# Moving the sections of G, splits, conversion and the state tile to other steps of a two-network kernel, and asking for later weights a phase earlier

## The chip, the cores and the metric

The kernel runs on one core of a Trainium2 chip. The metric is the device time of one execution in microseconds (us). Three runs of the kernel before gave 1648.82, 1658.09 and 1655.11 us, a median of 1655.11 us.

## The reference, cut to what matters

Three stages follow each other: an attention between 512 positions and 32 state slots for 4 batches of 8 heads, a mixture of 8 experts with a doubly normalised gate, and a gated two-layer network.

```python
# x: (4, 8, 512, 64), state: (4, 8, 32, 64)
a = softmax(x @ state.T / 8);   xread = a @ state
a2 = softmax(state @ x.T / 8);  sread = a2 @ x
x = concat([xread, sread], axis=2)          # to (2176, 512)
# experts: w1 (8, 512, 1024), w2 (8, 1024, 512)
P = exp(x @ w_gate - max); 8 times: rows to sum 1, columns to sum 1, times N / E
out = sum over e of P[:, e:e+1] * (relu(x @ w1[e]) @ w2[e])
# second network: w_in (512, 2048), w_out (2048, 512)
h = out @ w_in;  y = (h * sigmoid(h)) @ w_out
```

Inputs and outputs are float32, the second network's weights 64-bit. The kernel splits each operand into a high and a low part and multiplies three times (`mm3`, lines 91 to 93: high by low, low by high, high by high), which keeps float32 accuracy.

## The kernel before, in words

**Tiles and units.** Tokens come in batches `b` = 0 to 3 of 512 positions (four tiles of 128) and one tile `B` = 4 with the 128 state rows, called the state tile here. Each expert's hidden width of 1024 is cut into two units of 512, so there are 16 units `u` of four sections `f` of 128. One step `(u, b, f)` has a first layer `S1` (6 matmuls into a bank of the pool `p1`, then `hh` on ScalarE, L706, and `hl` on VectorE, L707) and a second layer `S2` (12 matmuls, three for each of the batch's four tiles, into four banks of the pool `p2`, tiles `po`). After the fourth section VectorE adds the four banks, weighted by the gate, to the accumulators (L746). `S1` runs two steps (`LAG`) ahead of `S2`. Units 0 and 1 do all four batches in this way. From unit 2 (`UPE`) on a unit does batches 0 and 1 alone, in eight steps, k = 4 b + f; batches 2 and 3 of these units come later, in a loop of their own with seven products for eight, for which GpSimd, ScalarE and the queues prepare sums of second weights during the dense units (`w2_sum`, `w2_split`).

**G.** The attention's read is a product with the state, so the first layer multiplies the attention weights by G = state x w1, which `g_pieces` makes: for each of four sections `hp` of 128 inputs 6 matmuls of 64 rows, two at a time on the two halves of the array (L626), into two banks; ScalarE copies the banks to a staging tile (L630) and sends it to memory, from where `load_g` and `split_g` bring it back in another order. `g_pair(u, i)` does two of the four sections, and so needs both banks of `p1` and both banks of `pm`. At units 2 and later the two pairs for unit u + 2 stand inside `S2`, after its second tile, at steps 1 and 2 (`within`).

**The state tile.** `sr_first(u)` is its first layer, 12 matmuls at once into a bank of `p1`; `sr_turn` transposes and splits the result; `sread_second` runs its four `S2` of three matmuls each, in step 3, in a bank of `p2`.

**Weights.** `load_raws` asks for a unit's raw weights in one tile of the pool `s8`; `load_w1` and `load_w2` split one section of them, high part on ScalarE (L243), low part on VectorE (L96, tile `l_w`). First weights for unit u + 3 are split at steps 5, 6, 7 and 0, second weights at 1, 2 for this unit and at 1, 6 for the next.

**Conversion.** The second network's weights are 64-bit words. `convert_some` advances a generator that turns them into high and low parts, mostly by VectorE (L302 to L360), and stores them; `store` issues the stores that have been put off. It is called at steps 2, 4, 5 and 6, and in the second network for the last quarter of the weights.

**The second network.** 16 phases `(g, v, fp)`: two halves `g` of the tokens, four quarters `v` of the width, two parts `fp`. A phase has seven `step(p)` (`product`, 6 matmuls, and the load of the next phase's weights) and, between them, four pieces `second(q - 1, n)` of the phase before. In the first half the state tile's part is interleaved: `s_first(v, half)` with weights `wr` from `s_load(v, half)`, `s_back`, `s_second`. `load_wout` asks for second weights, in a pool with five tiles for each of the two parts.

**What sets the order.** TensorE runs in the order written. The other engines' orders are made when the kernel is built: among instructions that are ready, the one written first goes first; a queue then runs in that order, and an instruction that waits holds up what is behind it. `behind_rows` and `issue_after` keep casts and conversion behind the last `hh` or `hl` written so far. SyncE issues nearly all loads, and most stores, from one queue.

Of the kernel before, what the change touches and what calls it, by code (L numbers as in the profile page):

```python
# [21 lines left out]
def fused_kernel(ctx: ExitStack, tc: tile.TileContext, x, state, w_gate, w1, w2, w_in, w_out, out):  # L22
# [16 lines left out]
    B, H, S, D = x.shape  # L39
    NS = state.shape[2]  # L40
    DM = H * D
    E, _, F = w1.shape
# [7 lines left out]
    NF = FU // 128  # L50
    KD = DM // 128
    UPE = F // FU
    NU = E * UPE
    NV = F2 // FU
# [26 lines left out]
    def p2(name):  # L81
        return ps2.tile([128, 512], F32, tag="p2", name=name)
# [287 lines left out]
    for v in range(NV):  # L370
        for kp in range(2):
            for j in range(2):
                k = kp + 2 * j
# [242 lines left out]
    def g_pieces(u, hps, banks):  # L616

        lanes = [slice(64 * half, 64 * half + 64) for half in range(2)]
        pg = {}
        for hp, bank in zip(hps, banks):  # L620
            wh, wl = w1t[u, hp]
            for half in range(2):
                pg[hp, half] = bank(f"pg{u}_{hp}_{half}")
            for i, (a, w) in enumerate(((stl, wh), (sth, wl), (sth, wh))):
                for half in range(2):
                    nc.tensor.matmul(pg[hp, half], a[lanes[half], hp], w[lanes[half]], start=i == 0, stop=i == 2)  # L626
        for hp in hps:
            stg = stp.tile([128, 2, FU], F32, tag="stg", name=f"stg{u}_{hp}")
            for half in range(2):
                nc.scalar.copy(stg[:, half], pg[hp, half])  # L630
            c = 2 * (hp & 1)
            nc.scalar.dma_start(out=g_d[u][hp // 2, c:c + 2].rearrange("h p f -> p h f"), in_=stg)
# [17 lines left out]
    def g_pair(u, i):  # L650
        if i == 0:
            g_start(u)
        g_pieces(u, (2 * i, 2 * i + 1), (pm, p1))

# [63 lines left out]
    def S2(u, b, f, within=()):  # L718
        tiles = batches[b]
        if f == 0:  # L720
            s2p[u, b] = [p2(f"po{u}_{b}_{t}") for t in tiles]
        hh, hl = hT.pop((u, b, f))
# [280 lines left out]
    def s_load(v, half):  # L1003
        pool, tag = (s8, "s8") if v else (accp, "acc")
        t = wr[v, half] = pool.tile([128, 2, 2, FU], F32R, tag=tag, name=f"wr_{v}_{half}")
        nc.sync.dma_start(out=t.bitcast(F32), in_=wr_d[v][2 * half:2 * half + 2].rearrange("k p s f -> p k s f"))
# [76 lines left out]

    pair_at = {0: {8: (1, 0), 9: (1, 1)}, 1: {6: (2, 0), 8: (2, 1), 13: (3, 0), 15: (3, 1)}, 2: {3: (4, 0), 4: (4, 1)}}

# [44 lines left out]
    bal = balance()  # L1130
    for i in range(-LAG, len(steps)):
        if i + LAG < len(steps):
            S1(*steps[i + LAG])
        else:
            block(UPE, 0, 0, i + LAG - len(steps))
# [3 lines left out]
        if i >= 0:  # L1139
            u, b, f = steps[i]  # L1140
            k = b * NF + f
            at = pair_at.get(u, {1: (u + 2, 0), 2: (u + 2, 1)}).get(k)
            if at and at[0] >= NU:
                at = None
            S2(u, b, f, [lambda: g_pair(*at)] if at else [])
        if i < B * NF:
# [37 lines left out]
        if late and k in (0, 1):  # L1184
            load_w1(4, 2 * k)
            load_w1(4, 2 * k + 1)
        if u > UPE and k in (1, 2):
            load_w2(u, k + 1)
        if u > UPE + 1 and k == 0 and u + 2 < NU:
            load_w1(u + 2, 3)  # L1190
        if k == 3:
            sread_second(u)
        store()
        if more and not late and k in (2, 4, 5, 6):
            convert_some()
# [8 lines left out]
        if more:  # L1204
# [5 lines left out]
            if k == 6:  # L1210
                if u + 2 < NU:
                    load_raws(2, u + 2)
                if u + 4 < NU:
                    load_raws(1, u + 4)
            if k == (5 if late else 4) and u + 2 < NU:
                sr_first(u + 2)
            if k == 6:
                sr_turn(u + 1)
            if k == (4 if late else 1):
                load_w2(u + 1, 0)  # L1220
# [4 lines left out]
            if u + 3 < NU:  # L1225
                for hp in ({6: (0, 1), 7: (2, 3)} if late else {5: (0,), 6: (1,), 7: (2,)}).get(k, ()):
                    load_w1(u + 3, hp)
# [117 lines left out]
    for q, (g, v, fp) in enumerate(phases):  # L1345
# [3 lines left out]
        def step(p):  # L1349
            product(q, p)  # L1350
            if more:
                load_win(*phases[q + 1][1:], p)
            if q < 6:
                store()
                if p in (2, 7) or q and p in (1, 5):
                    convert_some(1)
            if q == 7 and p != 4:
                later = {1: 6, 5: 3, 2: 7, 6: 4}.get(p)
                if later:
                    tokens(1, later)  # L1360
# [12 lines left out]
        if q == 0:  # L1373
            load_wout(0, 0, 2)
            s_first(0, 1)
            s_load(1, 0)
        elif g == 0 and fp == 1:
            s_back(v)
        step(6)
        earlier[1]()  # L1380
        if s0 and q:
            s_first(v, 0)
            s_load(v, 1)
        step(3)
        step(7)
        earlier[2]()
        if s0 and q:
            s_first(v, 1)
            if v + 1 < NV:
                s_load(v + 1, 0)  # L1390
        step(4)
        earlier[3]()
        if q == 0:
            load_wout(0, 0, 3)
        if more:
            for f in range(2):
                g1, v1, fp1 = phases[q + 1]
                if q:
                    load_wout(g1, v1, 2 * fp1 + f)
        if q == 6:  # L1400
# [39 lines left out]
```

## Time and profile before

| what | value |
|---|---|
| median of three runs | 1655.11 us |
| lowest, highest | 1648.82, 1658.09 us |
| profiled execution, its time | 1654.59 us |
| its span, first to last instruction | 1652.8 us |
| mean granted TensorE clock | 0.996 |
| TensorE busy | 1615.0 us (98%) |
| VectorE busy | 1098.7 us (66%) |
| ScalarE, GpSimd busy | 724.6 us (44%), 652.0 us (39%) |

The profiled execution is one run of the program; its time is 1.8 us longer than its span, for what lies around the first and last instruction. Busy shares are means over stages: start-up to about 100 us, units 0 and 1 to about 250 us, dense units to about 820 us, the other batches of those units to about 1280 us, the second network to the end. A window's column of busy time is followed by the number of instructions in brackets; PEclk is the granted clock as a share of 2.4 GHz.

### The profile page before, as it was taken

Reading aid. Unit: us, or ns where it says so; the run is one execution under the profiler, and the core shown is the slowest. Engines: PE = TensorE matmul, PEld = TensorE weight load, DVE = VectorE, ACT = ScalarE, POOL = GpSimd, SP = SyncE. Lnnn points to the kernel's source line nnn. Section 1 sums busy time; section 2 is a strip of 40 time slices with the busy share of each in tenths; the row PEclk is TensorE's granted clock in tenths of the full one; section 3 lists DMA queues with packets and bytes.
Section 4 is the critical chain, followed back from the end, with each engine's and each line's share of the span. In section 5 each row is a group of like instructions: output and inputs, shape, how many; then the busy total and the mean of one; then the engine's idle time right before and its main releaser. Section 6 shows DMA issues by size and latency. Waiting matters only on the chain.

```text
span 1652.8 us, 21117 instructions
## 1 busy us (share of the span) xinstructions
PE 1615.0 (98%) x7269; PEld 1291.5 (78%) x7269; DVE 1098.7 (66%) x1672; ACT 724.6 (44%) x1231; POOL 652.0 (39%) x487
## 2 busy tenths in 40 slices
PE   7999999999999999999999999999999999999998
PEld 5778777777777777777878788888888778888887
DVE  8933793567566666666447777777777878764554
ACT  5643346444444444343344444444444433443332
POOL 1001124444334423343457786776654512222222
PEclk9999999999999999999999999999999999999999
DMA  7043367676668656666356565454442787555441
GB/s 185 16 149 91 115 211 271 236 237 210 207 231 267 217 200 218 227 206 221 102 157 172 174 167 161 133 178 149 129 148 77 259 276 257 169 159 168 141 140 68
DMA packets 196395, 293.50 MB, mean 178 GB/s; under 512 B 35584, under 2 KB 82240, under 8 KB 196288
## 3 DMA queue, kind: packets, MB, share of 16 engines
q1 hardware_dynamic: 169552, 242.71, 47.5%
q10 hardware_dynamic: 26736, 49.44, 8.0%
q8 instruction: 58, 0.95, 0.2%
q14 instruction: 49, 0.40, 0.1%
HBM read 194.27 MB, written 97.81 MB: 177 GB/s over the span
## 4 chain that ended last, share of the span: by engine, by line
PE 84%; DVE 10%; DMA 2%; issue 1%; ACT 1%; POOL 1%; SPq 0%; DVEq 0%; ACTq 0%; POOLq 0%
PE pBa L984 9%; PE po L91 8%; PE po L93 7%; PE po L92 7%; PE pBc L984 5%; PE pa L791 4%; PE ph L91 4%; PE ph L93 3%; PE ph L92 3%; PE pr L91 3%; PE pr L92 3%; PE pB L91 3%; PE pr L93 3%; PE pB L93 3%; PE pB L92 3%; PE pg L626 3%
## 5 line engine op out<-in xcount | busy, mean ns | idle before, releaser
L707 DVE SCALAR_TENSOR_TENSOR hl<-ph,hh 128x512 fp32r<-128x512 f32 x144 | 98.9, 687 | 212.2 <-ACT hh L706 211.8
L91 PE MATMUL po<-h_w,hl 128*128 128x512 f32 x576 | 230.6, 400 | 6.9 <-DVE acc L746 6.9
L93 PE MATMUL po<-h_w,hh 128*128 128x512 f32 x576 | 226.6, 393 | 0.0
L92 PE MATMUL po<-l_w,hh 128*128 128x512 f32 x576 | 226.3, 393 | 0.0
L706 ACT ACTIVATE hh<-ph 128x512 fp32r<-128x512 f32 x144 | 86.3, 599 | 279.3 <-PE ph L93 276.4
L96 POOL TENSOR_TENSOR gl<-sg,gh 128x512 fp32r<-128x512 f32 x64 | 86.8, 1358 | 261.3 <-ACT gh L824 254.4
L96 POOL TENSOR_TENSOR G<-gf,G 128x512 fp32r<-128x512 f32 x64 | 85.3, 1355 | 262.9 <-ACT G L667 231.6
L91 PEld LDWEIGHTS po<-h_w,hl 128*128 128x128 f32 x576 | 108.5, 188 | 43.1 <-issue 11.2
L96 POOL TENSOR_TENSOR T<-t,T 128x512 fp32r<-128x512 f32 x84 | 112.3, 1338 | 73.5 <-ACT T L947 73.0
L984 PE MATMUL pBa<-T,wh 128*128 128x512 f32 x448 | 139.4, 392 | 0.7 <-DVE T L96 0.7
L220 POOL TENSOR_TENSOR w2s<-w2s,w2h 128x512 fp32r<-128x512 f32 x56 | 79.8, 1426 | 149.1 <-ACT w2h L219 148.9
L93 PEld LDWEIGHTS po<-h_w,hh 128*128 128x128 f32 x576 | 108.5, 188 | 23.9
L92 PEld LDWEIGHTS po<-l_w,hh 128*128 128x128 f32 x576 | 108.8, 189 | 22.8 <-issue 0.2
L91 PE MATMUL ph<-aTh,G 128*128 128x512 f32 x288 | 118.1, 410 | 3.8 <-DVE hl L707 1.9
L947 ACT CAST T<-t 128x512 fp32r<-128x512 f32 x112 | 69.6, 621 | 115.0 <-DVE t L952 94.6
L92 PE MATMUL ph<-aTl,G 128*128 128x512 f32 x288 | 113.1, 393 | 0.8 <-DVE aTl L96 0.8
L93 PE MATMUL ph<-aTh,G 128*128 128x512 f32 x288 | 113.5, 394 | 0.0
L91 PE MATMUL pr<-woh,gl 128*128 128x512 f32 x256 | 100.6, 393 | 0.7 <-DVE res L850 0.7
L92 PE MATMUL pr<-wol,gh 128*128 128x512 f32 x256 | 100.2, 391 | 0.0
L93 PE MATMUL pr<-woh,gh 128*128 128x512 f32 x256 | 100.0, 391 | 0.0
L984 PEld LDWEIGHTS pBa<-T,wh 128*128 128x128 f32 x448 | 84.2, 188 | 19.9 <-DVE T L96 1.3
L791 PE MATMUL pa<-x,wi 128*128 128x512 f32 x372 | 98.0, 399 | 0.7 <-ACT u L795 0.7
(267 smaller groups left out, 3835.8 us busy)
## 6 DMA issues: line engine op xcount, KB each, us to landing
g_d<-stg ACTq DMA_DIRECT2D x60, 512.0 KB, 3.7
wi<-wi_d SPq DMA_DIRECT2D x108, 256.0 KB, 3.0
raw<-in_moe_w_dram SPq DMA_DIRECT2D x104, 256.0 KB, 5.1
gf<-g_d SPq DMA_DIRECT2D x128, 128.0 KB, 4.2
w_d<-w2h ACTq DMA_DIRECT2D x56, 256.0 KB, 3.0
w_d<-w2s SPq DMA_DIRECT2D x56, 256.0 KB, 2.2
gfs<-g_d SPq DMA_DIRECT2D x112, 128.0 KB, 4.0
wh<-w_d SPq DMA_DIRECT2D x56, 256.0 KB, 3.3
```

The source lines that it names most:

```text
L91: nc.tensor.matmul(ps, al, bh, start=first, stop=False)
L92: nc.tensor.matmul(ps, ah, bl, start=False, stop=False)
L93: nc.tensor.matmul(ps, ah, bh, start=False, stop=last)
L96: engine.tensor_tensor(out=lo, in0=src, in1=hi.bitcast(F32), op=ALU.subtract)
L220: nc.gpsimd.tensor_tensor(out=t.bitcast(F32R), in0=t, in1=hi.bitcast(F32), op=ALU.subtract)
L626: nc.tensor.matmul(pg[hp, half], a[lanes[half], hp], w[lanes[half]], start=i == 0, stop=i == 2)
L706: last["act"] = nc.scalar.activation(out=hh, in_=ph, func=AF.Relu)
L707: last["dve"] = nc.vector.scalar_tensor_tensor(out=hl, in0=ph, scalar=0.0, in1=hh.bitcast(F32), op0=ALU.max, op1=ALU.subtract)
L791: nc.tensor.matmul(ps, a, b, start=begin, stop=kp == 1 and i == 2, skip_group_check=True)
L947: nc.scalar.copy(hi, t)
L984: nc.tensor.matmul(ps, a, b, start=p in (1, 2, 5) and q == 0 and i == 0, stop=q == 1 and i == 2, skip_group_check=True)
```

## The change

Nothing that is computed changes. In the dense units: a pair of sections of G stands in front of the first layer that is issued in a batch's first step (steps 0 and 4, the second pair for unit u + 2 and the first for unit u + 3) and no longer inside S2 at steps 1 and 2; the order of its four banks is different; the state tile's second layer goes from step 3 to step 2 and into the pool `pm`; `sr_first` from step 4 to 1, `sr_turn` from 6 to 4; first weights are split at steps 2, 2, 5 and 6; second weights a step earlier, and one from step 1 to 4; conversion is called at steps 1, 2, 4 and 5. Unit 2 has times of its own. In the second network: half of the `wr` tiles come from the pool `acc`, and `wr` is asked for in the phase before; `load_wout` is called in the phase itself and not at the end of the phase before; the calls of conversion are spread over one more phase.

```diff
@@ -617,10 +617,10 @@
 
         lanes = [slice(64 * half, 64 * half + 64) for half in range(2)]
         pg = {}
-        for hp, bank in zip(hps, banks):
+        for n, hp in enumerate(hps):
             wh, wl = w1t[u, hp]
             for half in range(2):
-                pg[hp, half] = bank(f"pg{u}_{hp}_{half}")
+                pg[hp, half] = banks[n][half](f"pg{u}_{hp}_{half}")
             for i, (a, w) in enumerate(((stl, wh), (sth, wl), (sth, wh))):
                 for half in range(2):
                     nc.tensor.matmul(pg[hp, half], a[lanes[half], hp], w[lanes[half]], start=i == 0, stop=i == 2)
@@ -650,7 +650,7 @@
     def g_pair(u, i):
         if i == 0:
             g_start(u)
-        g_pieces(u, (2 * i, 2 * i + 1), (pm, p1))
+        g_pieces(u, (2 * i, 2 * i + 1), ((p1, pm), (pm, p1)))
 
     gf = {}
 
@@ -718,7 +718,7 @@
     def S2(u, b, f, within=()):
         tiles = batches[b]
         if f == 0:
-            s2p[u, b] = [p2(f"po{u}_{b}_{t}") for t in tiles]
+            s2p[u, b] = [(pm if b == B and u > UPE else p2)(f"po{u}_{b}_{t}") for t in tiles]
         hh, hl = hT.pop((u, b, f))
         wh, wl = w2t[u, f]
         for i, ps in enumerate(s2p[u, b]):
@@ -1001,7 +1001,7 @@
         sx["h"], sx["l"] = hi, lo
 
     def s_load(v, half):
-        pool, tag = (s8, "s8") if v else (accp, "acc")
+        pool, tag = (accp, "acc") if v == 0 or half else (s8, "s8")
         t = wr[v, half] = pool.tile([128, 2, 2, FU], F32R, tag=tag, name=f"wr_{v}_{half}")
         nc.sync.dma_start(out=t.bitcast(F32), in_=wr_d[v][2 * half:2 * half + 2].rearrange("k p s f -> p k s f"))
 
@@ -1081,7 +1081,9 @@
     first = {0: {4: [(1, 0), (1, 1)], 5: [(1, 2), (1, 3)], 9: [(0, 0), (0, 1)], 10: [(0, 2), (0, 3)], 14: [(1, 0), (1, 1)], 15: [(1, 2), (1, 3)]},
              1: {**{k: [(2, k - 2)] for k in range(2, 6)}, **{k: [(3, k - 9)] for k in range(9, 13)}}}
 
-    pair_at = {0: {8: (1, 0), 9: (1, 1)}, 1: {6: (2, 0), 8: (2, 1), 13: (3, 0), 15: (3, 1)}, 2: {3: (4, 0), 4: (4, 1)}}
+
+    pair_within = {0: {8: (1, 0), 9: (1, 1)}, 1: {6: (2, 0), 8: (2, 1), 13: (3, 0), 15: (3, 1)}}
+    pair_at = {0: {}, 1: {}, 2: {3: (4, 0), 4: (4, 1)}, 3: {0: (5, 0), 1: (5, 1), 4: (6, 0)}}
 
     ask_at = {0: {11: (1, 0), 13: (1, 1)}, 1: {0: (1, 2), 3: (1, 3), 11: (2, 0), 13: (2, 1)}}
     split_at = {0: {12: (1, 0), 15: (1, 1)}, 1: {2: (1, 2), 5: (1, 3), 13: (2, 0), 15: (2, 1)}}
@@ -1129,6 +1131,11 @@
 
     bal = balance()
     for i in range(-LAG, len(steps)):
+        if i >= 0:
+            u, b, f = steps[i]
+            at = pair_at.get(u, {0: (u + 2, 1), 4: (u + 3, 0)}).get(b * NF + f)
+            if at and at[0] < NU:
+                g_pair(*at)
         if i + LAG < len(steps):
             S1(*steps[i + LAG])
         else:
@@ -1137,12 +1144,8 @@
             for piece in early.get(i, ((), ()))[0]:
                 piece()
         if i >= 0:
-            u, b, f = steps[i]
-            k = b * NF + f
-            at = pair_at.get(u, {1: (u + 2, 0), 2: (u + 2, 1)}).get(k)
-            if at and at[0] >= NU:
-                at = None
-            S2(u, b, f, [lambda: g_pair(*at)] if at else [])
+            at = pair_within.get(u, {}).get(b * NF + f)
+            S2(*steps[i], [lambda: g_pair(*at)] if at else [])
         if i < B * NF:
             for piece in early.get(i, ((), ()))[1]:
                 piece()
@@ -1184,14 +1187,12 @@
         if late and k in (0, 1):
             load_w1(4, 2 * k)
             load_w1(4, 2 * k + 1)
-        if u > UPE and k in (1, 2):
-            load_w2(u, k + 1)
-        if u > UPE + 1 and k == 0 and u + 2 < NU:
-            load_w1(u + 2, 3)
-        if k == 3:
+        if u > UPE and k < 2:
+            load_w2(u, k + 2)
+        if k == (3 if late else 2):
             sread_second(u)
         store()
-        if more and not late and k in (2, 4, 5, 6):
+        if more and not late and k in (1, 2, 4, 5):
             convert_some()
         if late and k == 0:
             w2_sum(u, 4)
@@ -1212,18 +1213,18 @@
                     load_raws(2, u + 2)
                 if u + 4 < NU:
                     load_raws(1, u + 4)
-            if k == (5 if late else 4) and u + 2 < NU:
+            if k == (4 if late else 1) and u + 2 < NU:
                 sr_first(u + 2)
-            if k == 6:
+            if k == (6 if late else 4):
                 sr_turn(u + 1)
-            if k == (4 if late else 1):
+            if k == 4:
                 load_w2(u + 1, 0)
             if k == 6:
                 load_w2(u + 1, 1)
             if k in (3, 7):
                 split_g(u + 1, k // 7)
             if u + 3 < NU:
-                for hp in ({6: (0, 1), 7: (2, 3)} if late else {5: (0,), 6: (1,), 7: (2,)}).get(k, ()):
+                for hp in ({5: (0, 1), 6: (2, 3)} if late else {2: (0, 1), 5: (2,), 6: (3,)}).get(k, ()):
                     load_w1(u + 3, hp)
             at = k - 3 if late else k
             if at == 0:
@@ -1350,9 +1351,9 @@
             product(q, p)
             if more:
                 load_win(*phases[q + 1][1:], p)
-            if q < 6:
+            if q < 8:
                 store()
-                if p in (2, 7) or q and p in (1, 5):
+                if p in ((2, 7), *[(1, 2, 7)] * 4, *[(1, 5, 2, 7)] * 2, ())[q]:
                     convert_some(1)
             if q == 7 and p != 4:
                 later = {1: 6, 5: 3, 2: 7, 6: 4}.get(p)
@@ -1371,32 +1372,28 @@
         step(2)
         earlier[0]()
         if q == 0:
-            load_wout(0, 0, 2)
             s_first(0, 1)
-            s_load(1, 0)
         elif g == 0 and fp == 1:
             s_back(v)
+        if q:
+            load_wout(g, v, 2 * fp)
+        if g == 0 and fp == 1 and v + 1 < NV:
+            s_load(v + 1, 0)
         step(6)
         earlier[1]()
+        if q:
+            load_wout(g, v, 2 * fp + 1)
         if s0 and q:
             s_first(v, 0)
-            s_load(v, 1)
         step(3)
         step(7)
         earlier[2]()
         if s0 and q:
             s_first(v, 1)
-            if v + 1 < NV:
-                s_load(v + 1, 0)
+        if g == 0 and fp == 1 and v + 1 < NV:
+            s_load(v + 1, 1)
         step(4)
         earlier[3]()
-        if q == 0:
-            load_wout(0, 0, 3)
-        if more:
-            for f in range(2):
-                g1, v1, fp1 = phases[q + 1]
-                if q:
-                    load_wout(g1, v1, 2 * fp1 + f)
         if q == 6:
             for p, (pool, tag) in zip((1, 5, 2), ((s8, "s8"), (accp, "acc"), (accp, "acc"))):
                 tokens(1, p, pool, tag)
```

## Rows read from the trace of the kernel before

**Rows 1.** The page, part 1: span, busy time and instructions.

```profile
span 1652.8 us, 21117 instructions
PE 1615.0 (98%) x7269; PEld 1291.5 (78%) x7269; DVE 1098.7 (66%) x1672; ACT 724.6 (44%) x1231; POOL 652.0 (39%) x487
```

**Rows 2.** Waits of TensorE, whole span: total us, times, longest.

```profile
PE po L91 <- DVE acc L746: 8.6, 4, 2.7
PE psf L91 <- DMA wr<-wr_d: 3.5, 1, 3.5
PE ph L91 <- ACT stg L630: 0.9, 2, 0.6
```

**Rows 3.** Windows, one unit each: busy us (instructions) of each engine, PEclk, DMA.

```profile
432.20:475.20 43.00, 42.99 (x200) 33.79 (x198) 25.40 (x40) 19.79 (x36) 15.73 (x12) 1.00 0.69 233
561.20:608.50 47.30, 44.92 (x200) 34.88 (x198) 34.05 (x49) 19.41 (x36) 17.17 (x12) 0.96 0.64 211
```

**Rows 4.** Windows, unit 6: steps 1 to 4, step 5, steps 5 to 0.

```profile
429.00:455.00 26.00, 26.00 (x121) 19.84 (x120) 10.54 (x18) 11.21 (x20) 7.81 (x6) 1.00 0.61 211
455.00:459.20 4.20, 4.20 (x19) 3.39 (x19) 1.89 (x3) 3.16 (x5) 2.60 (x2) 1.00 0.93 317
455.00:472.00 17.00, 17.00 (x77) 13.94 (x77) 14.66 (x21) 8.55 (x14) 7.92 (x6) 1.00 0.81 265
```

**Rows 5.** Windows around the wait of `po` that ends at 600.8 us.

```profile
597.00:600.70 3.70, 1.42 (x7) 0.84 (x5) 3.70 (x5) 1.10 (x2) 3.62 (x3) 1.00 0.61 227
600.70:604.40 3.70, 3.60 (x9) 2.86 (x10) 3.70 (x7) 0.00 (x0) 0.00 (x0) 0.54 0.00 0
```

**Rows 6.** Groups, VectorE, 301.3 to 783.8 us: busy us, mean ns, idle.

```profile
L96 DVE TENSOR_TENSOR l_w<-raw,h_w 128x512 fp32r<-128x512 f32 x84 | 68.2, 825 | 0.0
L746 DVE SCALAR_TENSOR_TENSOR acc<-po,P,acc 128x512 f32<-128x512 f32 x88 | 60.8, 742 | 22.8 <-PE po L93 22.8
...
L305 DVE SCALAR_TENSOR_TENSOR cv<-raw,cv 128x512 uint32<-128x512 uint32 x20 | 21.3, 1064 | 0.3
...
L354 DVE TENSOR_TENSOR ws<-wb,ws 128x256 f32<-128x256 f32 x5 | 2.1, 417 | 0.0
```

**Rows 7.** Timelines of VectorE and GpSimd: start us, us, instruction, idle before.

```profile
398.95 0.43 DVE L303 TENSOR_SCALAR cv<-cv 128x512 f32<-128x512 f32 x1
...
590.05 1.51 DVE L303 TENSOR_SCALAR cv<-cv 128x512 f32<-128x512 f32 x1
...
589.54 1.74 POOL L220 TENSOR_TENSOR w2s<-w2s,w2h 128x512 fp32r<-128x512 f32 x1
```

**Rows 8.** Timelines of TensorE, ScalarE and VectorE around two pairs of sections.

```profile
431.85 0.50 PE L626 MATMUL pg<-h_w,stl 64*128 64x512 f32 x2
...
437.83 0.50 PE L626 MATMUL pg<-h_w,stl 64*128 64x512 f32 x2
...
439.43 0.50 PE L91 MATMUL po<-h_w,hl 128*128 128x512 f32 x1
...
433.20 1.56 ACT L630 COPY stg<-pg 128x512 f32<-128x512 f32 x3 [0.45 <-PE pg L626]
...
438.89 1.07 ACT L630 COPY stg<-pg 128x512 f32<-128x512 f32 x2 [0.69 <-PE pg L626]
...
444.81 0.68 DVE L707 SCALAR_TENSOR_TENSOR hl<-ph,hh 128x512 fp32r<-128x512 f32 x1
```

**Rows 9.** The load of `wr`: a window behind the wait, SyncE's issue, landing.

```profile
1342.40:1348.50 6.10, 6.06 (x14) 4.79 (x15) 2.39 (x3) 1.08 (x2) 0.46 (x1) 0.50 0.61 201
...
1334.52 0.42 SPq L1006 DMA_DIRECT2D wr<-wr_d  x1
...
DMA to landing us min/median/max: 4.8/5.1/7.9
```

**Rows 10.** SyncE's last issues of raw weights in unit 6; page, part 6.

```profile
455.35 2.36 SPq L258 DMA_DIRECT2D raw<-in_moe_w_dram  x2
...
raw<-in_moe_w_dram SPq DMA_DIRECT2D x104, 256.0 KB, 5.1
```

## The prediction

> **What bounds the kernel now.** I read the page first. Its first part shows TensorE busy for 1615.0 of 1652.8 us [rows 1]: everything else matters only where it makes TensorE wait, and 37.8 us is the most that reordering can bring, apart from lost clock. So the second view is the list of waits, cut to TensorE [rows 2]. Most of its entries belong to the start-up, which the diff hardly touches. Two stand in stages that the diff rewrites: second layers (`po`, L91) that wait for VectorE's accumulation (L746) of the batch before, four times, 8.6 us, and one wait of 3.5 us for a load of `wr` in the second network.
>
> The third view is windows. Between the first products with the state (L626) of two neighbouring units lie 43.0 us when nothing is late, and 47.3 us in the unit in which one of those waits falls [rows 3]. What makes VectorE late is seen by cutting one undisturbed unit in two: in its steps 1 to 4 VectorE is busy 10.54 of 26.0 us (41%), from step 5 to the next unit's step 0 14.66 of 17.0 us (86%) [rows 4]. The long steps, which hold the two sections of G, the state tile and `sr_first`, carry little vector work; the short ones carry two pieces of conversion, four splits of first weights, a split of second weights and the last accumulation. Any extra wait of VectorE there comes out as a wait of `po`.
>
> A wait also costs clock. After the 2.4 us wait at 600.8 us the granted clock is 0.54 of full in the next 3.7 us, and nine matmuls start where sixteen would [rows 5].
>
> **The change, part by part.** A step has 18 matmuls in 4.2 us, 0.233 us each [rows 4].
>
> *Sections of G (`g_pair`) from the middle of S2 at steps 1 and 2 to the front of S1 at steps 0 and 4.* No work is added: 24 pairs before and after from unit 2 on, each 1.60 us from its first matmul to the next one of full height [rows 8]. What changes is who waits. The first tile of a batch's last S2 is done nine matmuls, 2.1 us, before that S2 ends; the first bank is wanted again at once by the state tile after batch 0, and after one S1 (1.4 us) behind batch 1. With 0.74 us for an accumulation [rows 6], VectorE may be late by 2.1 - 0.7 = 1.4 us in the first place and 2.8 us in the second. After the change the state tile sits in another pool and a pair and an S1 stand in front of the next batch: 2.1 + 1.6 + 1.4 - 0.7 = 4.4 us in both places (2.8 us where no pair is left, at the start of unit 14). The three waits behind batch 1, of up to 2.7 us [rows 2], mean lateness up to 5.5 us, so this alone would leave about 1 us of the longest.
>
> *Conversion from step 6 to 1; first-weight splits from 5, 6, 7 and 0 to 2, 2, 5 and 6; second-weight splits a step earlier, one from 1 to 4; `sr_turn` from 6 to 4.* Fifteen groups of conversion instructions, L305 the first and L354 the last by size, add up to 134.4 us in eleven units, with four calls each: 134.4 / 44 = 3.05 us a call. A weight split (`l_w`) is 0.83 us [rows 6]; I take the split after `sr_turn`, of the same form, as long. Steps 5 to 0 lose 3.05 + 2 x 0.83 + 0.83 and gain 0.83: 14.66 - 4.7 = 10.0 us, in 17.0 + 1.6 = 18.6 us of TensorE time (54%). Steps 1 to 4 get them: 10.54 + 4.7 = 15.2 us in 26.0 - 1.6 = 24.4 us (62%). The lateness that made the waits is thus taken from its place and put where there is room. I take all four waits as gone: 8.6 us, a restart of about 0.15 us each (0.6), and the slow stretch after 600.8 us, nine matmuls in 3.7 us in place of 9 x 0.233 = 2.1 us, 1.6 us [rows 5]. That is 10.8 us; the windows check it for that one wait: 47.3 - 43.0 = 4.3 us against 2.4 + 0.15 + 1.6 [rows 3].
>
> *The new pair's own price, ScalarE.* S1 now follows the pair, and its bank is one that the pair used, to be copied out by ScalarE (L630). The new order of banks puts the first half in that bank, so it is free after one copy. In one pair ScalarE began 1.06 us after the pair (437.83 to 438.89); with about 0.59 us for a copy S1 could start after 1.65 us, 0.05 us late. In another it began 1.35 us after (431.85 to 433.20), so 1.94 us, 0.34 us late [rows 8]. With 0.05 us for the semaphore: 24 x 0.1 = 2.4 us to 24 x 0.4 = 9.6 us. I take 0.15 us, 3.6 us, as at the end of steps 3 and 7 ScalarE has had the whole step, and set against it the present waits of S1 for the same copies, 0.9 us [rows 2]: net 2.7 us.
>
> *The pair's own price, VectorE.* Its last bank is that of the S1 one step before, free when `hl` (L707) is written. In the undisturbed unit step 3 begins at 441.1 (S2's last six matmuls follow 439.43), so a pair in front of step 4 would begin at 445.3 and want that bank 0.8 us later, at 446.1; `hl` ends at 445.5 [rows 8]. 0.6 us is spare, less than the four accumulations had. Bounds: nothing, and 1.5 us in each of eleven units, 16 us. Steps 1 to 3 keep more than a third of VectorE free, so I am near the low end: 1 us in all.
>
> *First weights split at step 2.* ScalarE's cast and VectorE's split would block their queues if the raw weights were late. SyncE issues them by 457.7 us, in step 5, ahead of the step 6 where they are written [rows 10]; a transfer of that line lands in 5.1 us, at about 463; the next unit's step 2 begins after the step 0 that ends at 472.0 [rows 4] and a step 1 of 5.9 us, at 478. 15 us spare: nothing. The staging tiles go from four within 6 us to two at a time: nothing, or a small gain.
>
> *Second network.* The load of the second half of `wr` for v = 1 is issued at 1334.52 and takes up to 7.9 us; TensorE waits 3.5 us [rows 2, 9]. Fourteen matmuls at a granted clock of 0.50 follow, 6.1 us in place of 14 x 0.233 = 3.3 us: 2.8 us more [rows 9]. Asked for a phase (over 20 us) earlier it is there: 3.5 + 0.1 + 2.8 = 6.4 us. `load_wout` moves from the end of a phase to the middle of the next, still a whole phase before its use: nothing. The conversions of the last quarter are 22 calls as before, three a phase in place of four at first and four in the two last; the last write is issued in phase 6 and read in phase 7: nothing.
>
> **Sum.** 10.8 + 6.4 - 2.7 - 1 = 13.5 us. The profiled execution took 1654.59 us, so 1641.1; it lies 0.5 us below the median shown. I predict 1641 us.
>
> **A rule that speaks against it.** In the trace one conversion operation takes 0.43 us, and 1.51 us where it starts beside a GpSimd operation of 1.74 us [rows 7]. So a conversion's price depends on what GpSimd does in its step, and GpSimd's sums and splits of weights for the other batches belong to steps 0 to 5. The Trainium skill, SBUF — State Buffer, section "Who interferes with whom", says that a VectorE instruction with two inputs in SBUF, or in a two-port mode, is blocked for the whole of a GpSimd instruction that has the shared port. The trace agrees in size. By that rule, with every moved operation blocked once, some six operations x 1.1 us would come before step 4, and the time would be that of the first rival.
>
> **The rivals.**
>
> *The wait moves to the new pair (other side).* VectorE comes late to step 4, by collisions such as 1.51 - 0.43 = 1.1 us, and the pair waits for `hl`. For: only 0.6 us is spare, and steps 1 to 3 receive most of the moved work. Against: `l_w` is 0.83 us in the mean of 84 [rows 6], so most do not collide, and 38% of those steps is free. Six collisions, 6.6 us, less 0.6 and the idle time of steps 2 and 3 (about 2 us) leave up to 4 us: 1640 + 11 x 4 = 1684, where 1640 is the sum without its 1 us for this. It decides from 2.1 us a unit: 11 x 2.1 = 23 us reaches 1663. At 1 us it is 1651.
>
> *ScalarE is late at every pair.* 0.4 us each, 9.6 us, nothing set against it: 1654.6 - 17.2 + 9.6 + 1 = 1648. For: S1 stands directly behind the pair. Against: ScalarE does 11.21 us in the 26.0 us of steps 1 to 4 [rows 4].
>
> *The early `wr` does not come early.* The pool that now takes it also holds two result tiles for the whole first half; were its request stuck behind a tile, or SyncE's queue stopped before it, the 6.4 us stay: 1647.5. Against: two of the four tiles of that pool are free after the first phase.
>
> *VectorE is late for another cause than its load*, and two of the four waits remain at about 1 us: 1643.
>
> **How the numbers follow.** The forecast, the last rival with it: 0.64. The pair waiting: 0.12 at 1 us a unit, within 0.5%, and 0.10 beyond 2.1 us. ScalarE late: 0.07, no change. `wr` not early: 0.07, on the bound, half to each side. 0.5% of the median, 8.3 us, is about what a measurement of this kernel can tell from no change: faster is below 1646.8, slower above 1663.4. Faster 0.64 + 0.03 = 0.67, same 0.12 + 0.07 + 0.04 = 0.23, slower 0.10. The range: the low end, 1632, has all 17.2 and 0.9 us gone at no price (1636.5), and 4 us of spread, less than the 6 by which the lowest run shown lies below the median; the high end, 1653, takes in a pair that waits 1 us a unit. The forecast's own is 1634 to 1646.
>
> **What would show it.** Right: no wait of `po` for L746 after unit 3, no unit over 44 us, none for `wr`, VectorE's busy share in steps 1 to 4 above that in steps 5 to 0, and matmuls at half clock gone at both places. Wrong: a wait of `pg` (L626) for `hl`, or of `ph` for L630, that comes back every unit; a ScalarE cast of first weights that waits for its DMA in step 2; the `wr` load issued late again; `pr` waiting for L850 in phases 5 to 7, where four conversion calls a phase now fall together with the next half's token tiles.

## The result and the profile after

The changed kernel takes 1631.55 us (median of four runs, 1630.54 to 1634.31) against 1651.96 us before (four runs, 1648.25 to 1658.09): a ratio of 0.9875, 95% interval 0.9838 to 0.9913. On another chip, with the experiments of the last group below, it came out again at 1632.27 us and 0.9867 (0.9847 to 0.9886). The forecast was 1641 us, its range 1632 to 1653: faster, as said, but by 20 us where 13.5 were summed, so that the median lies 0.45 us under the low end of the range. Between the two profiled executions, on which the sum was made, it is 1654.59 - 1630.70 = 23.9 us (24.3 us of span).

The page, part 1, of the changed kernel; it answers to [rows 1]:

```profile
span 1628.5 us, 21136 instructions
PE 1604.9 (99%) x7269; PEld 1290.3 (79%) x7269; DVE 1098.3 (67%) x1672; ACT 725.1 (45%) x1231; POOL 646.9 (40%) x487
```

TensorE runs the same 7269 matmuls and is busy 10.1 us less, with a mean granted clock of 0.999 where it was 0.996. VectorE's busy time, 1098.3 us, is the same within 0.4 us.

TensorE's waits in the changed kernel (total us, times, longest), to be read against [rows 2]. These four lie behind the start-up, and each is under 1 us; most of the others belong to the start-up, as before:

```profile
PE pg L626 <- DVE hl L707: 0.8, 1, 0.8
...
PE pr L91 <- DVE res L850: 0.7, 3, 0.2
...
PE px L761 <- DVE accs L746: 0.4, 1, 0.4
...
PE pB L91 <- POOL G L96: 0.2, 1, 0.2
```

The four waits of `po` for the accumulation (8.6 us) and the wait for `wr` (3.5 us) are gone, and those of S1 for the copies at L630 too. From 270 to 800 us the list is empty.

Windows of the changed kernel: three whole units (6, 9 and 10), from the pair of one step 0 to the next; then unit 6 cut as in [rows 4], steps 1 to 4 and steps 5 to 0. Columns as in [rows 3].

```profile
421.90:464.73 42.83, 42.80 (x198) 33.92 (x198) 27.66 (x41) 19.73 (x34) 16.14 (x13) 1.00 0.70 233
550.39:593.23 42.84, 42.81 (x197) 33.91 (x196) 31.00 (x50) 19.30 (x34) 16.40 (x13) 1.00 0.70 233
593.23:636.06 42.83, 42.80 (x197) 33.91 (x197) 26.29 (x41) 19.32 (x34) 16.29 (x13) 1.00 0.68 221
427.85:452.20 24.35, 24.35 (x113) 19.32 (x112) 13.43 (x21) 10.63 (x18) 9.70 (x8) 1.00 0.55 184
452.20:470.69 18.49, 18.46 (x88) 14.59 (x86) 14.24 (x19) 9.10 (x16) 6.44 (x5) 1.00 1.03 327
```

Units 4 to 10 take the same time, 42.83 us, where it was 43.0 when nothing was late and up to 47.3 when something was. The second window is the unit that was disturbed in [rows 3]: in both kernels it has more work for VectorE than its neighbours (50 instructions here and 49 there, where the others shown have 40 or 41), and nothing waits for it any more. The two stretches are as long as forecast (24.4 and 18.6 us), but VectorE's load in them is not: forecast were 15.2 and 10.0 us for unit 6. Unit 6 was also a poor sample. The sums of such windows over six units before (steps 1 to 4, then 5 to 0) and seven units after, with the mean of a window at the end (before, those of units 4 and 5 lie up to 1.9 us beside their steps, and the last one ends with the wait; over whole steps 5 to 0 of six units without a wait there the mean is 14.4 us, so the reading holds):

```profile
sum 156.00, PE 154.30 PEld 117.42 DVE 86.07 ACT 68.33 POOL 52.09; mean PE 25.72 PEld 19.57 DVE 14.34 ACT 11.39 POOL 8.68
...
sum 102.00, PE 99.62 PEld 81.50 DVE 87.25 ACT 49.37 POOL 48.44; mean PE 16.60 PEld 13.58 DVE 14.54 ACT 8.23 POOL 8.07
```

```profile
sum 170.45, PE 170.45 PEld 135.27 DVE 113.61 ACT 72.45 POOL 67.50; mean PE 24.35 PEld 19.32 DVE 16.23 ACT 10.35 POOL 9.64
...
sum 129.42, PE 129.21 PEld 102.18 DVE 91.59 ACT 64.14 POOL 45.61; mean PE 18.46 PEld 14.60 DVE 13.08 ACT 9.16 POOL 6.52
```

Steps 5 to 0 went from 14.54 of 17.0 us (86%) to 13.08 of 18.49 (71%), steps 1 to 4 from 14.34 of 26.0 (55%) to 16.23 of 24.35 (67%). The change took about 1.5 us from the crowded stretch, not 4.7.

The pair in front of step 4 of unit 6, and the first matmuls of the next pair and of the S1 behind it; timelines of TensorE, ScalarE and VectorE (start us, us, instruction, idle before):

```profile
445.64 0.39 PE L93 MATMUL po<-h_w,hh 128*128 128x512 f32 x1
445.95 0.50 PE L626 MATMUL pg<-h_w,stl 64*128 64x512 f32 x2
...
447.60 0.50 PE L91 MATMUL ph<-aTh,G 128*128 128x512 f32 x1
...
464.73 0.50 PE L626 MATMUL pg<-h_w,stl 64*128 64x512 f32 x2
...
466.43 0.50 PE L91 MATMUL ph<-aTh,G 128*128 128x512 f32 x1
...
446.96 1.07 ACT L630 COPY stg<-pg 128x512 f32<-128x512 f32 x2 [1.61 <-PE pg L626]
...
443.93 0.69 DVE L707 SCALAR_TENSOR_TENSOR hl<-ph,hh 128x512 fp32r<-128x512 f32 x1 [1.27 <-ACT hh L706]
```

S1 starts 1.65 us after the pair's first matmul, where 1.60 is a pair alone [rows 8]: the 0.05 us worked out for a ScalarE that is ready. At the next pair, in front of step 0, it is 1.70 us, 0.1 us late. `hl` ended at 444.62, 1.3 us before the pair begins.

SyncE's issue of the load that was late, and its time to landing (shortest, median, longest of three), against [rows 9]:

```profile
1293.57 0.43 SPq L1006 DMA_DIRECT2D wr<-wr_d  x1
...
DMA to landing us min/median/max: 6.1/7.4/8.3
```

The products that read it start at 1321.71 us: 28 us after the issue, more than three times the longest landing.

**Where the 24.3 us of span come from**, by setting the starts of the same matmuls in both executions side by side: 1.2 us before unit 2; 14.9 us in the units from 2 on, of which 11.0 at the four waits with their slow clock (1.85, 4.3, 2.8 and 2.06) and 3.8 elsewhere; 0.4 in the other batches; 7.6 in the second network, 6.4 of them at the wait for `wr`.

### The profile page after: what moved, and what is told of

Read it like the earlier page. It is cut to its first block, busy times and chain, and to the rows that moved or that the text cites. A ratio compares the mean times of both kernels' runs of the same rounds, so it can differ in the third digit from the quotient of the medians.

```text
span 1628.5 us, 21136 instructions
## 1 busy us (share of the span) xinstructions
PE 1604.9 (99%) x7269; PEld 1290.3 (79%) x7269; DVE 1098.3 (67%) x1672; ACT 725.1 (45%) x1231; POOL 646.9 (40%) x487
## 4 chain that ended last, share of the span: by engine, by line
PE 88%; DVE 6%; DMA 2%; ACT 1%; issue 1%; POOL 1%; SPq 1%; DVEq 0%; POOLq 0%; ACTq 0%
PE pBa L984 9%; PE po L91 8%; PE po L93 8%; PE po L92 8%; PE pa L791 5%; PE pBc L984 4%; PE ph L91 4%; PE ph L93 4%; PE ph L92 4%; PE pr L91 3%; PE pr L92 3%; PE pr L93 3%; PE pB L91 3%; PE pB L93 3%; PE pB L92 3%; PE pg L626 3%
## 5 line engine op out<-in xcount | busy, mean ns | idle before, releaser
L91 PE MATMUL po<-h_w,hl 128*128 128x512 f32 x576 | 226.7, 394 | 0.0
L791 PE MATMUL pa<-x,wi 128*128 128x512 f32 x372 | 96.8, 395 | 0.7 <-ACT u L795 0.7
```

The source lines that it names most:

```text
L91: nc.tensor.matmul(ps, al, bh, start=first, stop=False)
L791: nc.tensor.matmul(ps, a, b, start=begin, stop=kp == 1 and i == 2, skip_group_check=True)
```

## The experiments

All ratios are to the kernel before, run on the same chip (medians 1652.4 to 1652.7 us), with 95% intervals.

**1 and 2. The two halves of the change alone.** The first keeps every edit to the dense units and leaves the second network as before; the second keeps the edits to the second network alone, these lines among them:

```diff
-        pool, tag = (s8, "s8") if v else (accp, "acc")
+        pool, tag = (accp, "acc") if v == 0 or half else (s8, "s8")
...
-            if q < 6:
+            if q < 8:
                 store()
-                if p in (2, 7) or q and p in (1, 5):
+                if p in ((2, 7), *[(1, 2, 7)] * 4, *[(1, 5, 2, 7)] * 2, ())[q]:
...
+        if q:
+            load_wout(g, v, 2 * fp)
+        if g == 0 and fp == 1 and v + 1 < NV:
+            s_load(v + 1, 0)
```

> The change in the dense units alone; the second network is as before. Theory (the two parts are independent, and the dense part is worth the four waits of 10.8 us and some 4 us of small ones): about 16 us faster than before, ratio 0.990; no wait of po for L746, the wait of psf for wr (3.5 us) still there with matmuls at half clock behind it. Rival (the late wr of the second network follows from lateness that the dense units hand on, so that the dense part cures both): 22 to 24 us faster, ratio 0.986, no wait for wr.

Measured: 1638.48 us, 0.9924 (0.9898 to 0.9950), 14 us less where 16 were expected.

> The change in the second network alone; the dense units are as before. Theory: 7 us faster than before (6.4 us for wr and its slow clock, under 1 us of small waits), ratio 0.996; the waits of po for L746 stay, 8 to 9 us in all. Rival (as above): no gain, ratio 0.999 or more, since wr would still be late.

Measured: 1644.46 us, 0.9950 (0.9934 to 0.9966), 8 us less where 7 were expected. The waits of TensorE in each, 1 then 2:

```profile
PE psf L91 <- DMA wr<-wr_d: 6.7, 2, 4.9
```

```profile
PE po L91 <- DVE acc L746: 6.1, 4, 2.2
```

Each half keeps the other's wait and loses its own. The gains, 14 and 8 us, add up to the 20.4 us of the whole within 1.5 us: the halves are independent as far as this can tell, and the rivals are out.

**3. The pairs of steps 0 and 4 inside S2 again**, all else as changed:

```diff
-        if i >= 0:
-            u, b, f = steps[i]
-            at = pair_at.get(u, {0: (u + 2, 1), 4: (u + 3, 0)}).get(b * NF + f)
-            if at and at[0] < NU:
-                g_pair(*at)
...
-            at = pair_within.get(u, {}).get(b * NF + f)
+            u, b, f = steps[i]
+            at = pair_within.get(u, {}).get(b * NF + f) or pair_at.get(u, {0: (u + 2, 1), 4: (u + 3, 0)}).get(b * NF + f)
+            if at and at[0] >= NU:
+                at = None
```

> The changed kernel, with the pairs of sections of G at the same steps 0 and 4 but inside S2, after its second tile, as before. Theory (the lighter load of VectorE in steps 5 to 0 removes the waits; the place of the pair is worth little): 2 to 4 us slower than the changed kernel, by 0.2 us a unit and one or two short waits of po. Rival (the pair in front of S1 gives VectorE the time, and that removes the waits): 8 to 11 us slower, with waits of po for L746 back in three or four units.

Measured: 1628.78 us (1628.46 to 1631.31), 0.9865 (0.9847 to 0.9883). Both expectations have the wrong sign: without the front place no wait comes back. Whether it is faster than the changed kernel was settled on one chip, in experiments 9 and 10.

**4. The conversion back at its old steps**, all else as changed:

```diff
-        if more and not late and k in (1, 2, 4, 5):
+        if more and not late and k in (2, 4, 5, 6):
```

> The changed kernel, with conversion called at steps 2, 4, 5 and 6 as before. Theory (VectorE's load in steps 5 to 0 is the cause, but the first-weight splits and the pair in front give enough room by themselves): 0 to 3 us slower than the changed kernel, a wait of po under 1 us in one or two units. Rival (the conversion at step 6 is the whole cause): 8 to 11 us slower, three waits of po of 2 us or more.

Measured: 1643.99 us (median of five runs, 1639.73 to 1644.83; a sixth took 4498.94 us), 0.9942 (0.9922 to 0.9963), 12 us more than the changed kernel, just beyond the rival's 8 to 11 and far from the theory's 0 to 3. TensorE's waits from 270 to 800 us, the longest of them in its timeline, and a window behind it:

```profile
PE pg L626 <- DVE hl L707: 5.4, 3, 3.3
PE po L91 <- DVE acc L746: 1.8, 2, 1.0
...
688.53 0.79 PE L626 MATMUL pg<-h_w,stl 64*128 64x512 f32 x1 [3.34 <-DVE hl L707]
...
688.50:692.20 3.70, 3.67 (x10) 2.54 (x11) 3.70 (x6) 2.08 (x5) 1.28 (x1) 0.50 0.64 214
```

The waits are back, most at a new place: the pair in front of S1, on `hl`. That is the mechanism of the rival on the other side. It decides as soon as the conversion stands near it, and half the clock follows (0.50). Eight microseconds before the wait VectorE had stood idle for its data, and longer still in the kernel before, 9 us ahead of the longest of the four waits, that of 2.66 us at 691.46 us (here, then before):

```profile
680.29 0.43 DVE L302 TENSOR_SCALAR cv<-raw 128x512 uint32<-128x512 uint32 x1 [2.91 <-DMA raw<-in_moe_w_in_dram]
```

```profile
682.26 0.43 DVE L302 TENSOR_SCALAR cv<-raw 128x512 uint32<-128x512 uint32 x1 [5.34 <-DMA raw<-in_moe_w_in_dram]
```

In the kernel before, the same kind of wait took 7.8 us in all, three times; the changed kernel has none. From 682.26 us to the accumulations VectorE works without a break, so 5.34 us earlier it would not have been late. The dense units are the same in experiments 8, 2 and, but for the banks, 7: there this idle time is 2.61, 3.65 and 4.92 us, and the wait behind it 0.92, 1.38 and 2.67 us. One of the four waits, the longest, thus came from a conversion that was asked of VectorE before its raw weights had landed, more than from the amount of its work.

**5. The conversion's new steps alone**, on the kernel before (the line of experiment 4, the other way round).

> The kernel before, with conversion called at steps 1, 2, 4 and 5 of the dense units in place of 2, 4, 5 and 6; nothing else. Theory (the call at step 6 stands before the short steps, and its move is what removes the waits): the three waits of po behind batch 1 vanish, the one of the state tile behind batch 0 stays or grows, since a call more stands in front of it; 4 to 9 us faster than before, ratio 0.995 to 0.998. Rival (the move only pays together with the pairs, splits and state tile, as the place that it goes to has no room yet): as many waits in other places, of po in the state tile or of pg for hl at steps 1 and 2; ratio 0.999 to 1.002.

Measured: 1646.42 us, 0.9962 (0.9948 to 0.9975). 6 us less, as the theory had it, and the state tile's wait, which was to stay, is gone too. No `po` waits for VectorE, at the old places with their 1.4 and 2.8 us of slack. What is left from 300 to 800 us:

```profile
PE ph L91 <- ACT stg L630: 1.4, 5, 0.4
PE pg L626 <- DVE hl L707: 0.6, 1, 0.6
```

VectorE's share of steps 5 to 0 does not tell whether it is late: in unit 9 of this run it is busy 14.73 of 16.95 us there, more than the 14.4 of the kernel before, and nothing waits. That leaves what stands in its queue just in front of the accumulations, from where the call of step 6 is gone.

**6. The changed kernel with the old order of the pairs' banks.**

```diff
-        g_pieces(u, (2 * i, 2 * i + 1), ((p1, pm), (pm, p1)))
+        g_pieces(u, (2 * i, 2 * i + 1), ((pm, pm), (p1, p1)))
```

> The changed kernel, with the pairs' banks in the old order (first section of G in pm, second in p1). Theory (S1 behind the pair waits for the copy of the first bank of p1 that the pair filled: that is the first copy in the new order, the third in the old): 1.0 us more at each of 24 pairs, 20 to 24 us slower than the changed kernel, close to the kernel before. Rival (ScalarE's copies are hidden anyway): 0 to 3 us slower than the changed kernel.

Measured: 1669.17 us, 1.0104 (1.0077 to 1.0130): 38 us more than the changed kernel, nearly twice the expected (both expectations fail, the theory in size alone). In front of S1 the new order is a condition, not a refinement. Its waits, and one of them with ScalarE's copies beside it:

```profile
PE ph L91 <- ACT stg L630: 37.5, 26, 1.6
...
465.81 0.50 PE L91 MATMUL ph<-aTh,G 128*128 128x512 f32 x1 [1.50 <-ACT stg L630]
...
463.65 1.07 ACT L630 COPY stg<-pg 128x512 f32<-128x512 f32 x2 [1.61 <-PE pg L626]
...
465.17 1.07 ACT L630 COPY stg<-pg 128x512 f32<-128x512 f32 x2 [0.45 <-ACT stg L630]
```

S1's bank is the third to be copied in the old order, the first in the new.

**7. The new order of banks alone**, on the kernel before.

> The kernel before, with the pairs' banks in the new order alone; the pairs stay inside S2 at steps 1 and 2. Theory (part of what the sum missed is a wait of S1 for the copies in every unit of the kernel before, and longer ones in units 0 and 1): 0.2 us a unit and 1 to 2 us in units 0 and 1 less, 3 to 4 us faster, ratio 0.998. Rival (those waits are hidden elsewhere): ratio 1.000.

Measured: 1643.40 us, 0.9948 (0.9929 to 0.9968), 9 us and not 3 or 4. A clean unit, and the waits from 270 to 800 us:

```profile
429.40:472.15 42.75, 42.75 (x198) 33.93 (x197) 25.89 (x41) 19.77 (x35) 16.04 (x12) 1.00 0.72 234
...
PE po L91 <- DVE acc L746: 6.5, 3, 2.7
```

Against 42.99 us in a clean unit of the kernel before [rows 3]: 0.24 us a unit, from pauses that are too short each to stand in the list of waits. That makes 3 us in thirteen units. Of the other 6, about 2 are the `po` wait at 402 us, which no longer falls, and 1.3 to 1.8 lie in units 1 to 3; the rest was not traced. The size is loose: units 2 to 15, as they stand before, take 608.1, 603.9 and 607.4 us in the profiled executions of the kernel before and of experiments 2 and 8, and 600.5 us here.

**8. `wr` alone asked early**, on the kernel before.

> The kernel before, with wr asked for a phase earlier and half of it in the pool acc; nothing else of the second network. Theory (the late wr and the clock lost behind it are the second network's gain): no wait of psf, 6 to 7 us faster than before, ratio 0.996. Rival (the early wout loads and the spread of conversion bring a good part): a wait of psf or of pr stays, under 4 us faster, ratio 0.998 or more.

Measured: 1648.99 us, 0.9972 (0.9953 to 0.9991): some 4 us, by the interval 1.5 to 8, which does not decide between the two expectations. No wait for `wr`; two small ones come in its place, of `pa` for ScalarE and, in this row, of `prs` for VectorE:

```profile
PE prs L91 <- DVE res L852: 1.1, 2, 0.9
```

The traces tell more. From the first matmul of L791 to the end the second network takes 369.95 us in the kernel before, 365.11 here and 362.75 in experiment 2. So `wr` brings 4.8 us, and the spread conversion with the moved `load_wout`, where the small waits are absent, another 2.4.

**9 to 11. On one chip: the changed kernel again, experiment 3 again, and three edits alone.** The third of these is the kernel before with the conversion's new steps, the new bank order and the second network (experiments 5, 7 and 2 together); pairs, splits, state tile and loads of the dense units stay where they were.

> The changed kernel as it stands, on the chip that runs the next two, so that they can be set beside it. Both theories: 1630 to 1633 us, 20 us under the kernel before.

> The changed kernel with the pairs of steps 0 and 4 put inside the second layer of their steps again, beside the changed kernel on one chip. Theory (the place in front of the first layer costs TensorE 0.1 to 0.15 us a unit in pauses for copies and saves no wait): 1.5 to 3 us under the changed kernel, and its own fast end under the other's. Rival (the 2.8 us between the earlier two medians was the chip's): within 1 us of the changed kernel.

> The kernel before with three edits of the change: the conversion at steps 1, 2, 4 and 5, the new order of the pairs' banks, and all that the change does in the second network. The pairs stay at steps 1 and 2 inside the second layer, the splits, the state's tile and the weight loads of the dense units stay where they were. Theory (these three hold the whole gain, the pairs' new steps add nothing): no wait of a matmul for VectorE's sums in the dense units, and 1627 to 1633 us, level with the changed kernel. Rival (the conversion and the banks each took the same waits away, and the pairs' earlier steps with their longer slack are needed for the rest): matmuls wait 2 to 6 us for the low half of the hidden tiles or for the sums, and 1634 to 1640 us.

| kernel | us | runs | ratio to before |
|---|---|---|---|
| changed | 1632.27 | 1631.35 to 1632.47 | 0.9867 (0.9847 to 0.9886) |
| pairs inside S2 | 1629.59 | 1627.93 to 1630.87 | 0.9850 (0.9829 to 0.9871) |
| three edits | 1633.52 | 1633.29 to 1633.96 | 0.9875 (0.9855 to 0.9895) |

The runs of the three do not overlap. Units of the first, of the second, then of the third, one clean and two with a wait:

```profile
422.67:465.44 42.77, 42.74 (x198) 33.92 (x197) 27.61 (x41) 19.73 (x34) 16.12 (x13) 1.00 0.70 230
```

```profile
424.00:466.66 42.66, 42.66 (x198) 33.94 (x197) 28.94 (x41) 19.91 (x34) 16.58 (x13) 1.00 0.72 235
```

```profile
470.47:513.22 42.75, 42.75 (x199) 33.93 (x198) 29.36 (x44) 20.17 (x36) 16.19 (x12) 1.00 0.79 252
383.94:427.75 43.81, 43.23 (x198) 34.02 (x197) 34.59 (x50) 19.42 (x35) 17.02 (x12) 1.00 0.68 234
641.45:685.14 43.69, 43.19 (x197) 34.04 (x197) 32.59 (x46) 20.27 (x36) 16.98 (x12) 1.00 0.74 241
```

Three edits hold 19.2 of the 20.5 us: for the gain the theory stands, though the median lies 0.5 us above its range. Alone the three brought 6, 9 and 8 us, so they overlap (the wait at 402 us, for one, goes with either of the first two). The rest of the change, the pairs' steps with the splits, the state tile and the loads, is worth 1.3 us more: two small waits (0.6 us for `hl`, 0.5 for a copy), whose units are 1.06 and 0.94 us longer than a clean one, are absent. A clean unit costs the same on this chip, 42.77 us against 42.75. With the pairs left at steps 0 and 4 but put inside S2, there are no such waits either, a unit takes 42.66 us, and the median is 2.7 us less than that of the change as made. That version beats both kernels, by 23 and 2.7 us. Of the 2.7 us the place of the pair explains a part: over units 2 to 15 the two traces differ by 1.3 us (592.5 and 591.3), and the rest lies in stages in which the two kernels are written the same.

## Why the prediction fell short: the step that failed, and those that held

**The four waits, 10.8 us: right in size.** 11.0 us with the matmuls set side by side, the one at 600.8 us 4.3 us as worked out. Which part of the work makes VectorE late was right as well: the conversion's place is enough by itself to take the waits away (experiment 5), and putting it back brings waits back although the allowed lateness is now 4.4 us (experiment 4). Wrong was the working of the load. The splits did not leave the crowded stretch: over whole steps, 4.9 a unit ran in steps 5 to 0 before and after (34 in seven units both times). By the diff one of five should have gone, but the one now written at step 4 runs in step 5 (454.37 us in unit 6), and so does the split behind `sr_turn` (453.77). And the share did not fall to 54% but to 71%, so that the sign given for it, steps 1 to 4 fuller than steps 5 to 0, did not show. Nor is the load the whole cause: the longest wait came from raw weights that had not landed (5.34 us of idle VectorE), which is the last rival, VectorE late for another cause, and that wait went by luck, as far as the prediction goes: the moved calls find their words there (no such wait in the changed kernel). The slack was misjudged too: the pairs' move was to leave about 1 us of the longest wait, but experiment 4 shows 7.2 us with it, as the pair, which waits for `hl`, is late where `po` no longer is.

**`wr`, 6.4 us: right** at its place, 6.4 with the matmuls set side by side. Alone it brings 4.8 us in the traces, as small waits take its place, which the sum did not foresee.

**The price of the pairs, 2.7 + 1 = 3.7 us, is the step that failed.** In its place the units gained 3.8 us beyond the four waits. ScalarE's gross price of 3.6 us was too high: it is 0.05 and 0.10 us at the two pairs of unit 6, 0.11 us a unit on one chip (42.77 against 42.66), 1.3 us over all units. What was set against it, S1's 0.9 us of present waits, was far too little: its two waits lie before 300 us, and the list leaves out all shorter ones, which come in every unit. The order of banks gives back 0.24 us in each clean unit (experiment 7), and in experiment 7 the run-in of units 1 to 3 besides. VectorE's 1 us at the pair did not occur: no wait for `hl` after unit 1. That is 7.5 us of the 10.4 between forecast and profiled run. About 1 us of the 3.8 is seen in the clean units 4 to 10, some 0.15 us each (42.99 to 42.83); the rest lies in units 2 and 3 and from unit 11 on, and what brings it there was not traced. What is left of the 10.4 us the sum left out: 1.2 us in the first two units and 1.6 us of small waits in the second network and the other batches.

**Nothing for the splits at step 2, for `load_wout` and for the last quarter's conversion:** from 300 to 760 us no cast and no split of weights waits for its load, and `pr` waits 0.7 us in all, as before.

**The rivals.** The pair that waits for `hl` did not come in the changed kernel, but it is what experiment 4 shows, so the danger was real and the conversion's step decides it. ScalarE late at every pair is experiment 6: real too, with the old banks. The collisions that the first rival needed do occur. VectorE in steps 1 and 2 of unit 6 after, and GpSimd beside it:

```profile
431.27 0.42 DVE L351 TENSOR_TENSOR ws<-wb 128x256 f32<-128x256 f32 x1
431.73 1.51 DVE L352 TENSOR_TENSOR ws<-ws,wb 128x256 f32<-128x256 f32 x1
436.97 0.69 DVE L707 SCALAR_TENSOR_TENSOR hl<-ph,hh 128x512 fp32r<-128x512 f32 x1 [3.74 <-ACT hh L706]
...
431.66 1.29 POOL L220 TENSOR_TENSOR w2s<-w2s,w2h 128x512 fp32r<-128x512 f32 x1 [6.97 <-ACT w2h L219]
```

An operation on 256 columns takes 1.51 us beside GpSimd's 1.29, where one of the same size took 0.42 just before. The Trainium skill, SBUF — State Buffer, section "Who interferes with whom", says that such a VectorE instruction, with two inputs in SBUF, is held by a GpSimd instruction that reads there; this row agrees, as VectorE's ends 0.3 us after GpSimd's. But the 1.1 us vanish in the 3.74 us in which VectorE then waits for ScalarE. Such gaps in the steps that received the conversion fit a price of nothing; this is argued from this one place.

Not settled: why the order of banks alone removes the wait at 402 us, and how much of the 12 us of experiment 4 is the raw weights' load and how much the rest of VectorE's work.

## What to carry to other kernels

When a list of waits names one engine's lateness, look at what stands in its queue in front of the late instruction and whether it waits for data there, and move its optional work first: here one line, the steps of the conversion, removes all four waits, while in experiment 4 a longer slack for the waiting instruction only moved them to the next buffer that the late engine frees. Take the price of pauses that are too short for the list from a whole period of the steady state (42.99, 42.75, 42.66 us), which shows 0.1 us a unit. The changed kernel reads 42.83 and 42.77 us in two executions, so much less than that is not shown. And try each part of a change apart: the bank order alone was worth 9 us on the kernel before, and the place in front of the first layer cost 1.3 us or more.

## What the runs showed of the hardware that was not expected

A wait of 2.38 us at 600.8 us was followed by a clock of 0.54 [rows 5], most of that stretch at the lower level of 1.2 GHz; a longer one at 691.46 us in the same execution was not. Windows of the kernel before, the wait and what follows:

```profile
688.80:691.50 2.70, 0.04 (x2) 0.04 (x1) 2.70 (x6) 2.70 (x6) 1.18 (x1) 1.00 1.06 321
691.50:695.20 3.70, 3.70 (x16) 2.98 (x17) 3.70 (x6) 0.27 (x1) 2.62 (x3) 1.00 0.16 46
```

Sixteen matmuls start in 3.7 us at full clock, where nine did after the shorter wait. Nor does the clock fall behind the same wait in experiment 7, 2.37 us at 597.35 us (1.00 in the 3.7 us that follow), while it does in experiment 8 behind one of 1.82 us at 777.86 us (0.64). The length of a wait alone does not tell whether the clock falls.

With the waits much of the spread between runs went too: the kernel before ranges over 9.8 us in four runs, the changed one over 3.8 and, on the second chip, 1.1 us in five; the three edits over 0.7 us in four. Each half of the change alone, with the other half's wait left, keeps 11.8 and 9.6 us. Why is not shown.
